# A retention layer and two feed-forward layers on one core: first loads split in two, small tables through ScalarE's queue, decay factors per chunk, eight warm-up matmuls

## The chip, the cores and the metric

The kernel runs on one core of one Trainium2 chip. The metric is the device time of one execution in microseconds (us); of several executions the median is taken. One further execution was recorded by the hardware profiler: its span is the time from its first to its last profiled instruction. The engines are called as in the profile: PE (TensorE matmuls), PEld (its weight loads), DVE (VectorE), ACT (ScalarE), POOL (GpSimd) and SP (SyncE, which here only issues DMA transfers). A q behind a name (SPq, PEq) is the sequencer of that engine, which issues transfers and waits on semaphores.

## The reference, cut to what matters

Inputs are q, k and v of shape (4, 8, 576, 64) and the weights of two feed-forward layers. Everything is float32.

```
scores = (1/8) * q @ k^T                            # per batch and head, 576 x 576
Dmat   = gamma[h] ** (i - j) where i >= j, else 0   # gamma[h] = 1 - 2**(-5-h)
x      = (scores * Dmat) @ v                        # -> 2304 tokens x 512
h      = x @ w_in ;  x = (h * cos(h)) @ w_out       # 512 -> 2048 -> 512
xn     = x / sqrt(mean(x*x) + 1e-6) * rms_g
out    = (silu(xn @ w_gate) * (xn @ w_val)) @ w_out # 512 -> 1536 -> 512
```

## The kernel before

The attention with decay is computed in chunks. Each of the 4 batches of 576 positions has 4 full chunks of 128 positions and a rest of 64, which makes 20 chunks, numbered from 0; chunks 0 to 4 are the first batch. For one chunk the kernel loads four blocks of 128 x 512: `x[:, 0]` is k and `x[:, 1]` is q, both with the head dimension on the partitions, `x[:, 2]` is v and `x[:, 3]` is k again with the tokens on the partitions. In DRAM the four blocks lie side by side in each of the 128 rows, so that one partition's share of a chunk is one piece of 8 KB.

There are three small tables: `gk` (30 KB; decay factors of v in its first part, and in its second, `later`, one factor per head pair and chunk), `mask` (64 KB) and `gq` (256 KB, decay factors of q for the first chunk, which land in `gam0`). The factors of a later chunk c are `gam0` times a scalar from `later`; ScalarE makes them with four multiplications per chunk.

`scores(n)` multiplies v by its factors on POOL (L244), makes the products k q on PE into PSUM tiles `g` (L249), and masks them on DVE into `s` (L252). `values(n)` adds k v of this chunk to the running sum `total` in PSUM (L265), multiplies q by the `state` of the chunks before (L270, from the second chunk on), lets ScalarE copy `total` into `state` (L275), multiplies the masked scores by v (L280), and lets DVE multiply the result by the factors into `xall` (L283). The `g` tiles share three PSUM buffers. `total` of chunk n+1 is accumulated in the bank that the state copy of chunk n reads, so that the first L265 matmul of chunk 1 waits for the state copy of chunk 0.

Ahead of everything stand `WARM` matmuls on a tile of ones (`idle_bank`, L290), whose result nobody reads. The weights of the first feed-forward layer come in blocks of 1 MB (`raw`), and each is converted in several steps by ACT (L132, L141, L159) and DVE (L136, L137, L142, L143, L124). The first of these conversions, and the first products with them (L187 to L189), run between the chunks. That is also where the first layer's activation h cos(h) begins (L414 to L423). From the end of this mixed stage on the kernel is a long row of matmuls for the two feed-forward layers.

Up to the sixteenth step of the first feed-forward layer a scheduler puts the instructions of each engine into an order at build time, out of what it takes to be ready; the order in which the Python code calls the operations is only a priority there. Every engine then executes its own list strictly in that order, and waits on semaphores. Transfers go out in the order of the issuing engine's list, on 8 semaphores in turn: a transfer waits at issue until the one that last used its semaphore has landed. Before the change all transfers are issued by SP.

Of the kernel before, what the change touches and what calls it, by code (L numbers as in the profile page):

```python
# [22 lines left out]
F32 = mybir.dt.float32  # L23
# [3 lines left out]
AF = mybir.ActivationFunctionType  # L27
# [3 lines left out]
P = 128  # L31
# [6 lines left out]
NPAIR = H // 2  # L38
NFULL = S // P
REST = S - NFULL * P  # L40
NCH = NFULL + 1
# [18 lines left out]
NSLOT_B = NW1 - NSLOT_A  # L60
ATT_STEPS = 8
CONV_LEAD = 3
WARM = 10
AHEAD = 4
LAG = 3
LAST_BEGINS = [48, 51, 54, 65, 66, 67]
# [9 lines left out]
def body(ctx: ExitStack, tc, qkv, qkr, vr, w1, w2, rg, gq, gk, mask, out):  # L76
    nc = tc.nc
# [31 lines left out]
    def ps_tile():  # L109
        if "psh" not in late:  # L110
            return psa.tile([P, 512], F32, tag="g", bufs=3, name="g")
        taken[0] += 1
        return hidden_tile() if taken[0] % 2 else acc_tile(KC + taken[0] // 2 % 2)

    mask_sb = const.tile([P, P], F32, name="mask_sb")
# [51 lines left out]
    def temps():  # L167
        return cvp.tile([P, 2, 512], I32, tag="w", name="t")
# [6 lines left out]
    def split_x(t):  # L175
        t0, n = TILES[t]
        for kc in range(KC):
            hi = xsp.tile([P, 512], F32R, tag="xs", name="xhi")
            lo = xsp.tile([P, 512], F32R, tag="xs", name="xlo")
            src = xall[:, kc, t0:t0 + n]  # L180
            nc.scalar.copy(hi[:, :n], src)
            minus(nc.vector, lo[:, :n], hi[:, :n], src)
            xs[t, kc] = (hi, lo)
# [17 lines left out]
    ap1 = att.enter_context(tc.tile_pool(name="ap1", bufs=1, reuse_waits="tile"))  # L201
# [3 lines left out]
    width = lambda c: P if c < NFULL else REST  # L205
    ld, sc, total = {}, {}, {}
    gam0 = ap1.tile([P, NPAIR, P], F32, name="gam0")
    gam = [gam0]
    PRO = NCH
    gk_sb = ap1.tile([P, NCH * (H + NPAIR)], F32, name="gk_sb")  # L210
    vg_sb = gk_sb[:, :NCH * H].rearrange("p (c h) -> p c h", c=NCH)
    later = gk_sb[:, NCH * H:].rearrange("p (c a) -> p c a", c=NCH)
# [6 lines left out]
    def load(n):  # L219

        b, c = chunks[n]
        x = wa.tile([P, 4, DM], F32, tag="w", name="x")
        if n == 0:
            for src, dst in ((qkv[b, c, :, 0], x[:, 0]), (qkv[b, c, :, 1], x[:, 1]), (gk, gk_sb), (mask, mask_sb),
                             (qkv[b, c, :, 2], x[:, 2]), (gq, gam0), (qkv[b, c, :, 3], x[:, 3])):
                nc.sync.dma_start(dst, src)
        elif c < NFULL:
            nc.sync.dma_start(x, qkv[b, c])
        else:
            nc.sync.dma_start(x[:, :2, :NPAIR * REST], qkr[b])  # L230
            nc.sync.dma_start(x[:REST, 2], vr[b])
        blocks = lambda a: a[:, :NPAIR * width(c)].rearrange("p (a i) -> p a i", a=NPAIR)
        ld[n] = blocks(x[:, 0]), blocks(x[:, 1]), x[:, 2], x[:, 3]
        if 0 < n < NCH:
            gam.append(ap1.tile([P, NPAIR, width(c)], F32, name=f"gam{c}"))
            for p in range(NPAIR):
                nc.scalar.activation(gam[c][:, p, :], gam0[:, p, :width(c)], AF.Copy, scale=later[:, c, p:p + 1])

    def scores(n):
        b, c = chunks[n]  # L240
        w = width(c)
        kt, qt, vv, _ = ld[n]
        v3 = vv[:w].rearrange("p (h d) -> p h d", h=H)
        nc.gpsimd.tensor_tensor(v3, v3, vg_sb[:w, c, :].unsqueeze(2).to_broadcast([w, H, D]), op=ALU.mult)  # L244
        ps = [ps_tile().rearrange("p (h i) -> p h i", h=NPAIR) for _ in range(2)]
        for p in range(NPAIR):
            for hh in range(2):
                r = slice(hh * D, (hh + 1) * D)
                nc.tensor.matmul(ps[hh][:w, p, :w], kt[r, p, :], qt[r, p, :], start=True, stop=True)  # L249
        for hh in range(2):  # L250
            s = ap.tile([P, NPAIR, P], F32, tag=f"s{hh}", bufs=2, name=f"s{hh}")
            nc.vector.tensor_tensor(s[:w, :, :w], ps[hh][:w, :, :w],  # L252
                                    mask_sb[:w, :w].unsqueeze(1).to_broadcast([w, NPAIR, w]), op=ALU.mult)
            sc[n, hh] = s

    def values(n):
        b, c = chunks[n]
        w = width(c)
        _, qt, vv, kk = ld.pop(n)
        if c < NFULL:  # L260
            if c == 0:
                total[0] = psa.tile([P, NPAIR, P], F32, tag="st", name="total")
            for p in range(NPAIR):
                cs = slice(p * P, (p + 1) * P)
                nc.tensor.matmul(total[0][:, p, :], kk[:, cs], vv[:, cs], start=c == 0 and p == 0, stop=True,  # L265
                                 skip_group_check=True)
        po = ps_tile().rearrange("p (a i) -> p a i", a=NPAIR)
        if c > 0:
            for p in range(NPAIR):
                nc.tensor.matmul(po[:, p, :w], state[:, p, :], qt[:, p, :], start=p == 0, stop=False,  # L270
                                 skip_group_check=True)
        if c < NFULL:
            for hh in range(2):
                r = slice(hh * D, (hh + 1) * D)
                nc.scalar.copy(state[r, :, r], total[0][r, :, r])  # L275
        for p in range(NPAIR):
            for hh in range(2):
                h = 2 * p + hh
                r = slice(hh * D, (hh + 1) * D)
                nc.tensor.matmul(po[r, p, :w], vv[:w, h * D:(h + 1) * D], sc[n, hh][:w, p, :w],  # L280
                                 start=c == 0 and p == 0, stop=True, skip_group_check=True)
        t0 = b * S + c * P
        nc.vector.tensor_tensor(xall[:, :, t0:t0 + w], po[:, :, :w], gam[c], op=ALU.mult)  # L283
        del sc[n, 0], sc[n, 1]
# [3 lines left out]
    idle_bank = psp.tile([P, 512], F32, tag="acc0", name="idle_bank")  # L288
    for _ in range(WARM):
        nc.tensor.matmul(idle_bank, ones_r, warm, start=True, stop=True)  # L290
    plan = list(PLAN)

    def fetch(until):

        while plan and until not in ld:
            n = plan.pop(0)
            if n < 0:
                blocks1.append(Block(w1[len(blocks1)], wa))
            else:
                load(n)  # L300
# [3 lines left out]
    for n in range(PRO):  # L304
        fetch(n + AHEAD)
        scores(n + 1)
        values(n)
        if n == 3:
            split_x(ORDER_A[0])
            blocks1[0].convert(temps())  # L310
# [316 lines left out]
    for i in range(LAST + LAG):  # L627
# [12 lines left out]
        if i < LAST:  # L640
            t, f = steps[i]
# [278 lines left out]
```

## Time and profile before

| | |
|---|---|
| median of 3 runs | 930.67 us (929.98 to 932.38) |
| the profiled execution, device time | 928.54 us |
| its span | 926.7 us |
| PE busy in the span | 903.1 us (97%) |
| DVE busy | 619.6 us (67%) |
| ACT busy | 462.2 us (50%) |
| moved by the DMA engines | 163.72 MB, mean 177 GB/s |

Busy shares are means over the whole span; the change touches its first microseconds, which have to be read for themselves. The profiled execution's device time is 1.84 us above its span and 2.13 us below the median.

### The profile page before, as it was taken

Reading aid. Unit: us, or ns where it says so; the run is one execution under the profiler, and the core shown is the slowest. Engines: PE = TensorE matmul, PEld = TensorE weight load, DVE = VectorE, ACT = ScalarE, POOL = GpSimd, SP = SyncE. Lnnn points to the kernel's source line nnn. Section 1 sums busy time; section 2 is a strip of 40 time slices with the busy share of each in tenths; the row PEclk is TensorE's granted clock in tenths of the full one; section 3 lists DMA queues with packets and bytes.
Section 4 is the critical chain, followed back from the end, with each engine's and each line's share of the span. In section 5 each row is a group of like instructions: output and inputs, shape, how many; then the busy total and the mean of one; then the engine's idle time right before and its main releaser. Section 6 shows DMA issues by size and latency. Waiting matters only on the chain.

```text
span 926.7 us, 12891 instructions
## 1 busy us (share of the span) xinstructions
PE 903.1 (97%) x4996; PEld 791.0 (85%) x4996; DVE 619.6 (67%) x1022; ACT 462.2 (50%) x816; POOL 26.9 (3%) x27
## 2 busy tenths in 40 slices
PE   7999999999999999999999899999999999999998
PEld 6777788888887888988888799999888999999997
DVE  3999989778888887768657666675456446333332
ACT  4656566576556666367545444444432334322222
POOL 2321100000000000000000000000000000000000
PEclk9999999999999999999999999999999999999999
DMA  8946451035424353202035376676744555755531
GB/s 334 410 186 227 155 224 72 21 117 193 164 98 159 137 159 126 69 1 103 1 148 204 124 297 251 252 268 246 259 176 176 207 209 212 265 206 209 204 132 69
DMA packets 34732, 163.72 MB, mean 177 GB/s; under 512 B 4080, under 2 KB 5232, under 8 KB 23792
## 3 DMA queue, kind: packets, MB, share of 16 engines
q1 hardware_dynamic: 34672, 162.91, 48.0%
q8 instruction: 39, 0.64, 0.3%
q14 instruction: 21, 0.17, 0.1%
HBM read 123.57 MB, written 39.32 MB: 176 GB/s over the span
## 4 chain that ended last, share of the span: by engine, by line
PE 79%; DVE 14%; ACT 4%; issue 2%; DMA 1%; SPq 0%; ACTq 0%; DVEq 0%
PE h L743 27%; PE acc L715 15%; PE acc L187 8%; PE acc L188 8%; PE acc L189 8%; PE h L189 3%; PE h L188 3%; PE h L187 3%; DVE r L421 1%; DVE t L142 1%; DVE t L143 1%; PE g L280 1%; DVE r L415 1%; PE g L249 1%; PE g L270 1%
## 5 line engine op out<-in xcount | busy, mean ns | idle before, releaser
L743 PE MATMUL h<-w 128*128 128x384 f32 x1224 | 230.5, 337 | 6.6 <-ACT s L750 2.6
L743 PEld LDWEIGHTS h<-w 128*128 128x128 f32 x1224 | 214.9, 188 | 15.2 <-ACT s L750 5.3
L715 PE MATMUL acc<-w,shi 128*128 128x512 f32 x432 | 134.3, 392 | 0.0
L187 PE MATMUL acc<-ghi,w 128*128 128x512 f32 (+1 forms) x320 | 117.4, 373 | 2.8 <-ACT xall L614 1.7
L188 PE MATMUL acc<-glo,w 128*128 128x512 f32 (+1 forms) x320 | 117.6, 369 | 0.1
L189 PE MATMUL acc<-ghi,w 128*128 128x512 f32 (+1 forms) x320 | 117.3, 368 | 0.0
L750 ACT COPY s<-h 128x384 f32<-128x384 f32 x108 | 51.9, 480 | 128.1 <-PE h L743 128.0
L715 PEld LDWEIGHTS acc<-w,shi 128*128 128x128 f32 x432 | 80.1, 188 | 13.4
L417 ACT ACTIVATE r<-r,half_pi 128x512 f32<-128x512 f32 (+1 forms) x80 | 54.5, 681 | 65.5 <-DVE r L415 65.2
L763 DVE TENSOR_TENSOR sg<-s,h 128x384 f32<-128x384 f32 x54 | 29.9, 553 | 85.6 <-PE h L743 45.4
L715 PE MATMUL acc<-w,slo 128*128 128x512 f32 x216 | 85.4, 395 | 0.0
L775 ACT CAST shi<-v 128x384 fp32r<-128x384 f32 x72 | 37.0, 514 | 70.3 <-DVE v L771 70.3
L124 DVE TENSOR_TENSOR glo<-r,ghi 128x512 fp32r<-128x512 f32 (+1 forms) x78 | 49.6, 636 | 33.4 <-ACT ghi L423 31.6
L187 PEld LDWEIGHTS acc<-ghi,w 128*128 128x128 f32 x320 | 59.4, 188 | 14.5 <-ACT xall L614 2.8
L423 ACT CAST ghi<-r 128x512 fp32r<-128x512 f32 (+1 forms) x80 | 46.2, 577 | 48.2 <-DVE r L421 46.9
L189 PEld LDWEIGHTS acc<-ghi,w 128*128 128x128 f32 x320 | 60.3, 188 | 10.1
L188 PEld LDWEIGHTS acc<-glo,w 128*128 128x128 f32 x320 | 60.3, 188 | 10.1 <-DVE glo L124 0.3
L124 DVE TENSOR_TENSOR slo<-v,shi 128x384 fp32r<-128x384 f32 x72 | 40.1, 557 | 37.3 <-ACT shi L775 37.3
L770 DVE TENSOR_TENSOR v<-s,h 128x384 f32<-128x384 f32 x54 | 29.8, 552 | 52.0 <-PE h L743 37.9
L743 PE MATMUL h<-b,w 128*128 128x384 f32 x288 | 56.8, 338 | 0.0
L188 PE MATMUL h<-xlo,w 128*128 128x512 f32 (+1 forms) x148 | 54.3, 367 | 0.1
L189 PE MATMUL h<-xhi,w 128*128 128x512 f32 (+1 forms) x148 | 54.2, 366 | 0.0
(105 smaller groups left out, 1518.6 us busy)
## 6 DMA issues: line engine op xcount, KB each, us to landing
w<-s SPq DMA_DIRECT2D x24, 1024.0 KB, 4.8
raw<-w_dram SPq DMA_DIRECT2D x36, 512.0 KB, 4.0
w<-w SPq DMA_DIRECT2D x18, 1024.0 KB, 5.1
w<-s SPq DMA_DIRECT2D x24, 768.0 KB, 6.4
raw<-w_dram SPq DMA_DIRECT2D x16, 1024.0 KB, 7.1
x<-qkv_dram SPq DMA_DIRECT2D x15, 1024.0 KB, 8.1
s<-w SPq DMA_DIRECT2D x12, 1024.0 KB, 4.8
s<-w SPq DMA_DIRECT2D x12, 768.0 KB, 3.6
```

Of the source, the lines that this page charges most:

```text
L124: eng.tensor_tensor(dst, src, hi.bitcast(F32), op=ALU.subtract)
L187: nc.tensor.matmul(dst, a[0], b[0], start=start, stop=False)
L188: nc.tensor.matmul(dst, a[0], b[1], start=False, stop=False)
L189: nc.tensor.matmul(dst, a[1], b[0], start=False, stop=stop)
L417: nc.scalar.activation(r, r, AF.Sin, bias=half_pi, scale=1.0)
L423: nc.scalar.copy(hi, r)
L715: nc.tensor.matmul(acc, (hi, hi, lo)[k][:, c], w[:, u, (0, 1, 0)[k], :], start=start and u == 0 and k == 0, stop=stop and u == 1 and k == 2)
L743: nc.tensor.matmul(bank, a[:, wp], xp[:, c], start=start and kc == 0 and n == 0, stop=kc == 1 and n == 2, skip_group_check=True)
L750: nc.scalar.copy(t, alpha)
L763: nc.vector.tensor_tensor(t, s, bank, op=ALU.add)
L770: nc.vector.tensor_tensor(t, s, bank, op=ALU.add)
L775: nc.scalar.copy(hi, t)
```

## The change

The first chunk's four blocks come in two transfers of two blocks each, in place of four; the second chunk's come in two in place of one. The three tables are issued by ScalarE (`nc.scalar`) in place of SP. The four multiplications that make a chunk's decay factors are called when the previous chunk has been computed, in a function of their own, and no longer at the load. `WARM` is 8 in place of 10.

```diff
-WARM = 10
+WARM = 8
...
         if n == 0:
-            for src, dst in ((qkv[b, c, :, 0], x[:, 0]), (qkv[b, c, :, 1], x[:, 1]), (gk, gk_sb), (mask, mask_sb),
-                             (qkv[b, c, :, 2], x[:, 2]), (gq, gam0), (qkv[b, c, :, 3], x[:, 3])):
-                nc.sync.dma_start(dst, src)
+            for eng, src, dst in ((nc.sync, qkv[b, c, :, :2], x[:, :2]), (nc.scalar, gk, gk_sb),
+                                  (nc.scalar, mask, mask_sb), (nc.sync, qkv[b, c, :, 2:], x[:, 2:]),
+                                  (nc.scalar, gq, gam0)):
+                eng.dma_start(dst, src)
+        elif n == 1:
+            nc.sync.dma_start(x[:, :2], qkv[b, c, :, :2])
+            nc.sync.dma_start(x[:, 2:], qkv[b, c, :, 2:])
         elif c < NFULL:
             nc.sync.dma_start(x, qkv[b, c])
...
-        if 0 < n < NCH:
-            gam.append(ap1.tile([P, NPAIR, width(c)], F32, name=f"gam{c}"))
-            for p in range(NPAIR):
-                nc.scalar.activation(gam[c][:, p, :], gam0[:, p, :width(c)], AF.Copy, scale=later[:, c, p:p + 1])
+
+    def decay(c):
+
+        gam.append(ap1.tile([P, NPAIR, width(c)], F32, name=f"gam{c}"))
+        for p in range(NPAIR):
+            nc.scalar.activation(gam[c][:, p, :], gam0[:, p, :width(c)], AF.Copy, scale=later[:, c, p:p + 1])
...
         fetch(n + AHEAD)
         scores(n + 1)
         values(n)
+        if n + 1 < NCH:
+            decay(n + 1)
```

The scheduler puts the following rows at the start of ScalarE's list; before the change first (`gam` are the decay factors, `gam_91` the loaded table, `raw` and `t` belong to the first weight block):

```order
L237 ACT_TABLE_LOAD
L237 ACTIVATE gam_121<-gam_91,gk_sb 128x128 x4
L237 ACTIVATE gam_143<-gam_91,gk_sb 128x128 x4
L237 ACTIVATE gam_150<-gam_91,gk_sb 128x128 x4
L237 ACTIVATE gam_160<-gam_91,gk_sb 128x64 x4
L275 COPY state<-total 64x4x64 x4
L132 ACTIVATE t<-raw 128x1024
```

After the change ScalarE's list begins as follows (its line 243 is line 237 of before, and 281 is 275):

```order
L227 DMA gk_sb<-gk_dram 128x60
L227 DMA mask_sb<-mask_dram 128x128
L227 DMA gam_91<-gq_dram 128x512
L243 ACT_TABLE_LOAD
L243 ACTIVATE gam_174<-gam_91,gk_sb 128x128 x4
L243 ACTIVATE gam_216<-gam_91,gk_sb 128x128 x4
L243 ACTIVATE gam_260<-gam_91,gk_sb 128x128 x4
L243 ACTIVATE gam_302<-gam_91,gk_sb 128x64 x4
L281 COPY state<-total 64x4x64 x4
L132 ACTIVATE t<-raw 128x1024
```

Three transfers now stand ahead; the sixteen multiplications stand together as before, ahead of the first state copy, although they are called chunk by chunk.

PE's list begins so before the change (L249 are the scores, L265 the sum k v, L280 the masked scores times v):

```order
L290 MATMUL idle_bank<-warm,ones_r 128x512 x10
L249 MATMUL g<-x 128x128 x8
L265 MATMUL total<-x 128x128 x4
L249 MATMUL g<-x 128x128 x8
L280 MATMUL g<-s_137,x 64x128
...
L265 MATMUL total<-x 128x128 x2
L249 MATMUL g<-x 128x128 x8
L265 MATMUL total<-x 128x128 x2
L270 MATMUL g<-x,state 128x128 x4
```

And so after it (255 is 249, 271 is 265, 276 is 270, 286 is 280):

```order
L296 MATMUL idle_bank<-warm,ones_r 128x512 x8
L255 MATMUL g<-x 128x128 x16
L271 MATMUL total<-x 128x128 x4
L286 MATMUL g<-s_129,x 64x128
...
L271 MATMUL total<-x 128x128 x4
L255 MATMUL g<-x 128x128 x8
L276 MATMUL g<-x,state 128x128 x4
```

The scores of chunk 1 moved ahead of the sum of chunk 0, and the sum of chunk 1 is no longer split around the scores of chunk 2.

In DVE's list the rows of the first weight block and of chunks 2 to 5 stand so before the change:

```order
L252 TENSOR_TENSOR s_251<-g,mask_sb 128x512
L136 TENSOR_SCALAR t<-t 128x1024
L137 TENSOR_SCALAR t<-t 128x1024
L142 SCALAR_TENSOR_TENSOR t<-raw,t 128x1024
L283 TENSOR_TENSOR xall<-g,gam_143 128x4x128
L252 TENSOR_TENSOR s_286<-g,mask_sb 64x4x64
L252 TENSOR_TENSOR s_288<-g,mask_sb 64x4x64
L143 ISA t<-raw,t 128x2048
L283 TENSOR_TENSOR xall<-g,gam_150 128x4x128
```

And so after it (258 is 252, 289 is 283):

```order
L258 TENSOR_TENSOR s_238<-g,mask_sb 128x512
L136 TENSOR_SCALAR t<-t 128x1024
L137 TENSOR_SCALAR t<-t 128x1024
L289 TENSOR_TENSOR xall<-g,gam_216 128x4x128
L258 TENSOR_TENSOR s_278<-g,mask_sb 64x4x64
L258 TENSOR_TENSOR s_280<-g,mask_sb 64x4x64
L142 SCALAR_TENSOR_TENSOR t<-raw,t 128x1024
L143 ISA t<-raw,t 128x2048
L289 TENSOR_TENSOR xall<-g,gam_260 128x4x128
```

One step of the weight conversion moved behind three steps of the attention. Differences of this kind, a conversion step or a few matmuls that stand some places earlier or later, go on through the first quarter of DVE's list, the first fifth of ACT's and the first sixth of PE's; behind that the lists are the same.

## Rows read from the trace of the kernel before

**Rows 1.** The page: the span, and busy time of each engine.

```profile
span 926.7 us, 12891 instructions
PE 903.1 (97%) x4996; PEld 791.0 (85%) x4996; DVE 619.6 (67%) x1022; ACT 462.2 (50%) x816; POOL 26.9 (3%) x27
```

**Rows 2.** Windows: length, busy time (instructions) by engine, granted clock, DMA share, GB/s.

```profile
10.00:15.00 5.00, 2.59 (x36) 2.10 (x35) 1.89 (x3) 4.58 (x17) 2.08 (x2) 1.00 1.01 428
15.00:20.00 5.00, 5.00 (x64) 4.45 (x63) 1.98 (x3) 1.57 (x3) 1.04 (x1) 1.00 1.05 377
20.00:25.00 5.00, 4.92 (x61) 4.27 (x57) 4.72 (x7) 2.10 (x4) 2.62 (x2) 1.00 0.99 413
...
30.00:60.00 30.00, 27.37 (x212) 22.45 (x213) 29.36 (x37) 18.22 (x26) 7.19 (x6) 0.94 0.83 328
...
130.00:160.00 30.00, 30.00 (x136) 24.79 (x133) 29.64 (x39) 21.84 (x28) 0.00 (x0) 1.00 0.40 158
```

**Rows 3.** The chain that ended last, two pieces: start, length, what.

```profile
3.07 4.95 DMA gam<-gq_dram
...
14.75 0.68 PE total L265 x4
```

**Rows 4.** The timeline of the first 23 us: start, length, instruction [idle before <- releaser].

```profile
0.74 0.87 SPq L226 DMA_DIRECT2D x<-qkv_dram  x2
...
2.10 4.59 PE L290 MATMUL idle_bank<-warm,ones_r 128*128 128x512 f32 x10 [2.10 <-DVE warm L287]
...
3.07 0.43 SPq L226 DMA_DIRECT2D gam<-gq_dram  x1
...
4.02 1.54 SPq L228 DMA_DIRECT2D x<-qkv_dram  x3
...
6.62 1.16 PE L249 MATMUL g<-x 64*128 64x128 f32 x16
7.44 1.04 POOL L244 TENSOR_TENSOR x<-x,gk_sb 128x512 f32<-128x512 f32 x1 [6.51 <-DMA x<-qkv_dram]
...
8.10 1.28 ACT L237 ACT_TABLE_LOAD   x1 [8.10 <-DMA gam<-gq_dram]
...
9.03 1.13 PE L265 MATMUL total<-x 128*128 128x128 f32 x8 [1.25 <-DMA x<-qkv_dram]
9.39 4.57 ACT L237 ACTIVATE gam<-gam,gk_sb 128x128 f32<-128x128 f32 x16
...
11.48 1.16 PE L249 MATMUL g<-x 64*128 64x128 f32 x16 [1.32 <-DMA x<-qkv_dram]
...
12.57 1.09 PE L280 MATMUL g<-s,x 128*64 128x128 f32 x16
...
14.75 0.68 PE L265 MATMUL total<-x 128*128 128x128 f32 x4 [1.09 <-ACT state L275]
...
19.16 1.15 ACT L132 ACTIVATE t<-raw 128x1024 f32<-128x1024 f32 x1 [0.25 <-DMA raw<-w_dram]
...
22.25 0.76 ACT L275 COPY state<-total 64x256 f32<-64x256 f32 x2 [0.88 <-PE g L270]
```

**Rows 5.** DMA issues in short windows: size, us from issue to landing.

```profile
x<-qkv_dram SPq DMA_DIRECT2D x1, 256.0 KB, 3.0
...
gam<-gq_dram SPq DMA_DIRECT2D x1, 256.0 KB, 5.0
...
x<-qkv_dram SPq DMA_DIRECT2D x1, 1024.0 KB, 7.4
...
raw<-w_dram SPq DMA_DIRECT2D x1, 1024.0 KB, 13.5
```

**Rows 6.** Windows of 1 us in the first load phase (columns as in Rows 2).

```profile
2.00:3.00 1.00, 0.90 (x2) 0.83 (x3) 0.00 (x0) 0.00 (x0) 0.00 (x0) 1.00 0.75 260
...
5.00:6.00 1.00, 1.00 (x3) 0.79 (x3) 0.00 (x0) 0.00 (x0) 0.00 (x0) 1.00 0.87 203
```

**Rows 7.** One window with a lower granted clock (columns as in Rows 2).

```profile
33.90:37.30 3.40, 3.40 (x9) 2.63 (x9) 3.33 (x6) 0.17 (x1) 1.05 (x1) 0.51 1.03 411
```

## The prediction

> **What bounds the kernel now.** I read the page first. PE is busy for 903.1 of 926.7 us [rows 1], so all that any change can take out of this kernel, short of taking work from PE, is the 23.6 us in which PE has nothing to do. The question is how much of that lies where the change is made. The windows tell it. From 15 to 20 us PE is busy for the whole 5.00 us, and from 130 to 160 us for all of 30.00; in between DVE is the one that is full, with 29.36 of 30 us from 30 to 60 us [rows 2]. Before 15 us it is otherwise: from 10 to 15 us PE works for 2.59 us and DVE for 1.89, while ACT works for 4.58 [rows 2]. So the start is a stage of its own, and ends when PE becomes full at about 14.75 us.
>
> The chain of waits says what sets that moment. It goes from the issue of the table `gq` at 3.07 us, by its transfer of 4.95 us, through ACT to the matmul L265 that starts chunk 1's sum at 14.75 us [rows 3]. The timeline has the pieces: the table has landed at about 8.05 us, ACT loads its function table (8.10, 1.28 us), makes all sixteen products for the decay factors (9.39, 4.57 us), and only then, in the order of its list, copies the state, which the L265 row at 14.75 us names as its releaser [rows 4]. From landing to L265 that is 14.75 - 8.05 = 6.70 us. Everything else that chunk 1 needs stands ready: its scores ended at 12.64 us and L280 of chunk 0 at 13.66 [rows 4].
>
> From there each chunk hands on to the next, and nothing is tied to the clock on the wall but what the transfers bring. So if L265 of chunk 1 starts earlier by some amount, PE's full stretch starts earlier by that amount, DVE's full stretch behind it too, and so the end, as long as data and order allow. That is the sum that I make: the shift of this one moment.
>
> **The change part by part.**
>
> The tables through ScalarE. SP issues seven transfers of 0.42 to 0.44 us each for chunk 0 and the tables, and `gq` is the sixth, at 3.07 us [rows 4]. Now it is third in ACT's own list. If ACT starts at the same 0.74 us and needs the same time for an issue, `gq` goes out at 0.74 + 2 x 0.43 = 1.6 us. How long it then takes, no row shows, since ACT issues no transfer before. From below: the first `x` transfer has the same 256 KB and finds the engines empty, 3.0 us [rows 5], which gives 4.6 us. From above: `gq`'s own 5.0 us with five transfers ahead [rows 5], which gives 6.6. It will share the engines with 512 KB of chunk 0 ahead of it and 512 KB beside it, so neither row is clearly nearer, and I take the middle, 5.6 us. L265 then starts at 5.6 + 6.70 = 12.3 us in place of 14.75: a gain of 2.45 us, with 3.45 and 1.45 as its ends.
>
> Against the tables' new queue stands a rule of the Trainium skill, in the page "DMA: Bandwidth & Descriptors", section "Issuing engines are not separate DMA queues": transfers started by different engines run on the same 16 DMA engines and mix there, and a second issuing engine saves only the time of issue. By that rule the gain is at its lower end, 3.07 - 1.6 = 1.45 us, since only the issue moves.
>
> The decay factors per chunk. By the code ACT would make four products, copy the state, and go on. By the order it does not: all sixteen stand ahead of the first copy as before. This edit costs and gives nothing. Had it worked, twelve products (3.4 us of the 4.57) would have left the path, and PE's own work would have set the time.
>
> The loads in two transfers. x of chunk 0 goes out in two issues in place of four, and with the tables gone SP has issued chunk 0 and the whole of chunk 1 by 0.74 + 4 x 0.43 = 2.5 us; before, chunk 1 was issued at 4.02 us and landed 7.4 us later, at 11.4 [rows 4, 5]. In the first load phase, with rows of 2 KB and smaller, the engines moved 260 and 203 GB/s [rows 6], some 230; with rows of 8 KB they moved 428 [rows 2]. Rows of 4 KB do not occur before, so I take these as bounds. The first half of chunk 1 is ready when 1.57 MB of x and at most 0.36 MB of tables have moved from about 1.75 us on, the second half with 0.52 MB more: with some 0.5 us until the landing is seen, 6.8 to 10.6 us and 8.0 to 12.9 us. That this is early enough decides whether the 2.45 us stand. PE, in the new order, does the scores of chunk 0, the scores of chunk 1, the sum of chunk 0 and L280 of chunk 0, of 1.16, 1.16, 1.13 and 1.09 us [rows 4]: with the first half landed at 6.8 us it is done at 10.2, at 10.6 us at 14.0. POOL needs 1.04 us [rows 4] behind the second half, 9.0 to 13.9. In the middle of the ranges PE is done at 12.1 and POOL at 11.5, and ACT, at 12.3, is last, if by little. So the loads earn nothing by themselves, but cover the tables; at the slow end L265 would start at 14.0 us and the gain would shrink to 0.7 us.
>
> The first weight block sits behind the loads. It lands at 5.6 + 13.5 = 19.1 us, and ACT takes it up at 19.16 [rows 4, 5]; behind it on ACT stands the state copy of chunk 2, which today has 0.88 us of idle time before it [rows 4]. With 5.6 MB moved, of which 2.1 MB at 330 GB/s (the middle), 0.36 MB at 230 and 3.1 MB at 428, it now lands at about 17.4 us, 1.7 us earlier. With the 0.88 us this allows a shift of up to 2.6. The 2.45 just fit.
>
> Eight warm-up matmuls. Ten take 4.59 us [rows 4], so two are worth 0.9 us of PE time before the scores of chunk 0, which can begin at about 5.8 us. PE's path has 12.3 - 10.2 = 2.1 us of slack if chunk 1 is early, and waits for its transfer if it is late. Nothing comes of this edit either way, but for the clock, below.
>
> The new order behind 15 us. Some conversion steps and matmuls change places in a stretch in which PE and DVE are both close to full: from 30 to 60 us PE has 2.6 us free and DVE 0.6 [rows 2]. DVE's work is the same, so a gain is bounded by about that 0.6 us and what PE loses to a slow clock there; a loss is not bounded by a row. I put it at 0, and allow 1.5 us on either side, about half of PE's free time there.
>
> Sum: -2.45 us. The profiled execution would go from 928.54 to 926.1 us; set against the median, which is 2.13 us above that execution, 930.67 becomes **928.2 us**.
>
> **The rivals.** What a measurement of this kernel can tell from no change is about 0.3%, 2.8 us.
>
> First, small gain. The tables gain only their earlier issue, or chunk 1 comes late, or the new order gives a microsecond back. For it speaks that the engines are already 75 to 87% busy in the first load phase [rows 6], so that `gq` has to share with x wherever it is issued. The gain is 0.7 to 1.45 us, in the middle 1.1: 929.6 us.
>
> Second, larger gain. `gq` meets the lower end (3.45 us earlier), and the new order closes some of the 2.6 us of PE's holes from 30 to 60 us, among them the stretch from 33.9 to 37.3 us at a granted clock of 0.51, in which nine matmuls ran where the row from 130 to 160 us has 136 in 30 us, or 15 in 3.4 [rows 2, 7]: 926.3 us. Against it: the conversion of the first weight block allows about 2.6.
>
> Third, slower, by the clock. The granted clock fell to the lower level, 1.2 GHz, at 33.9 us, after a stretch in which PE had waited for ACT and DVE [rows 7]; and the ten warm-up matmuls went at 0.46 us each [rows 4] against 0.22 later [rows 2], so they ran at the lower level too, though the clock column has 1.00 there. With two fewer of them, and with chunk 1's scores now ahead of chunk 0's sum, PE may stand idle from about 7 us until the first half of chunk 1 lands. If the clock then stays at 1.2 GHz, the 9.3 us of matmuls from the scores of chunk 0 to L280 of chunk 1, which ended at 19.1 us, run at half pace until it rises at a time T, and end at 12.2 + T/2. Even with before is T = 13.8 us; 2.8 us slower, T = 19.4. At that point the time would be 933.5 us. Against it: before, PE idled for 1.09 to 1.32 us three times by 14.75 us [rows 4] and the clock held at 1.00 [rows 2]. The page "TensorE: Matmul & The Clock Gate" of the Trainium skill says, in its part 1, that the low clock is the idle state and that matmul activity lifts it; the trace agrees with the 0.46 and 0.22 us above.
>
> That the change does not do what it says holds for the decay factors, as said; it is in the sum.
>
> **How the numbers follow.** The forecast, a gain of 1.7 to 3.3 us, gets 0.42, the larger gain 0.24, the small one 0.22, slower or no gain by clock or order 0.12. The forecast's own range is 927.4 to 929.0 us; the part of it beyond 2.8 us is the smaller one, so 0.16 of the 0.42 counts as faster. Faster by over 0.3%: 0.16 + 0.24 = 0.40. Slower by over 0.3%: 0.08 of the 0.12. Within: 0.52. The range leaves out the far ends of the larger gain and most of slower: 925.0 to 931.4 us.
>
> **What would show it.** Right: in the changed trace `gq` lands near 5.6 us, the first state copy ends near 12.2 and names the last decay product ahead of it, L265 of chunk 1 starts near 12.3, and PE and DVE do at 27 us what they did at 30. The table load waits for `gq` alone. The two transfers of chunk 1 land by about 8.7 and 10.4 us. Wrong: L265 waits for POOL or a transfer; ACT stands before the weight block with the state copy behind it; a granted clock of 0.5 in the first 20 us; or PE's idle time from 20 to 130 us differs by more than 1.5 us, which would say that the order and not the start decided.

## The result, and the profile after

The changed kernel is slower: 937.97 us median of 6 runs (935.78 to 938.81) against 930.62 us (927.10 to 932.38), a ratio of 1.0076 [1.0059, 1.0094]. The forecast was 928.2 us (925.0 to 931.4). The profiled execution took 938.81 us, and its page begins so:

```profile
span 937.0 us, 12888 instructions
...
PE 907.4 (97%) x4994; PEld 794.7 (85%) x4994; DVE 621.5 (66%) x1022; ACT 462.0 (49%) x816; POOL 27.7 (3%) x27
```

The span is 10.3 us longer than in [rows 1], and PE is busy for only 4.3 us more. The rest is idle time of PE, so something waits. Some 3 us of the 10.3 belong to the two executions that were profiled: the one of before took 2.1 us less than its median, this one 0.8 us more than its own. The first place to look is where the change was made. The timeline of the changed kernel, its first 20 us (start, length, what, and in brackets the idle time before and what ended it):

```profile
1.62 0.45 ACTq L227 DMA_DIRECT2D gam<-gq_dram  x1
...
5.78 1.87 PE L255 MATMUL g<-x 64*128 64x128 f32 x16
...
8.57 1.28 ACT L243 ACT_TABLE_LOAD   x1 [8.57 <-DMA gam<-gq_dram]
9.02 1.16 PE L255 MATMUL g<-x 64*128 64x128 f32 x16 [1.37 <-DMA x<-qkv_dram]
...
9.87 4.57 ACT L243 ACTIVATE gam<-gam,gk_sb 128x128 f32<-128x128 f32 x16
...
14.34 0.74 ACT L281 COPY state<-total 64x256 f32<-64x256 f32 x2
15.18 1.13 PE L271 MATMUL total<-x 128*128 128x128 f32 x8 [2.89 <-issue]
...
19.36 1.15 ACT L132 ACTIVATE t<-raw 128x1024 f32<-128x1024 f32 x1
```

The table `gq` is issued at 1.62 us, as forecast, but ACT gets it only at about 8.5 us, where before it had it at 8.05 [rows 4]. From there the start runs as the prediction said, with all sixteen products in one row ahead of the state copy, and L271 of chunk 1 (L265 before) starts at 15.18 us in place of 14.75. The transfers of the first 25 us say why (KB each, median us from issue to landing):

```profile
gam<-gq_dram ACTq DMA_DIRECT2D x1, 256.0 KB, 6.9
...
mask_sb<-mask_dram ACTq DMA_DIRECT2D x1, 64.0 KB, 4.9
```

The table took 6.9 us from ScalarE's queue, where it took 5.0 from SP's [rows 5]. Its issue 1.45 us earlier is more than given back. Still, 0.4 us at the start is not 10. The windows (length, busy time and instructions of PE, PEld, DVE, ACT, POOL, granted clock, DMA share, GB/s) tell where the rest is:

```profile
10.00:15.00 5.00, 2.29 (x28) 1.82 (x24) 1.98 (x3) 4.97 (x18) 2.08 (x2) 1.00 1.01 426
15.00:20.00 5.00, 4.82 (x58) 4.32 (x59) 1.66 (x3) 1.45 (x4) 1.38 (x2) 1.00 1.04 364
20.00:25.00 5.00, 5.00 (x67) 4.52 (x64) 4.25 (x9) 2.29 (x4) 1.74 (x2) 1.00 1.00 418
...
30.00:60.00 30.00, 23.24 (x158) 18.36 (x160) 29.15 (x34) 16.95 (x23) 7.77 (x6) 0.92 0.73 281
60.00:90.00 30.00, 28.68 (x236) 23.68 (x235) 23.21 (x32) 15.73 (x24) 2.33 (x2) 0.85 0.50 176
```

Up to 25 us the rows look like those of before [rows 2]. From 30 to 60 us PE is busy for 23.24 us against 27.37, while DVE is full in both; from 60 to 90 us the clock is 0.85, where the same window of before has 29.96 us of PE at 1.00:

```profile
60.00:90.00 30.00, 29.96 (x267) 24.69 (x263) 28.82 (x39) 20.77 (x28) 4.61 (x4) 1.00 0.53 181
```

Over both windows PE is idle for 8.1 us against 2.7, which is 5.4 more, and the clock takes 0.08 x 30 + 0.15 x 30 = 6.9 us against 1.8, which is 5.1 more. Together 10.5 us: by this reckoning as much as the whole difference of the two spans lies between 30 and 90 us, where the prediction had put 0. The view of the waits names what PE waits for from 20 to 130 us (total, times, longest):

```profile
PE g L276 <- DVE s L258: 6.0, 3, 3.6
PE g L286 <- DVE s L258: 1.9, 1, 1.9
```

L258 is the masking of the scores on DVE (L252 before). The same view of before has these two kinds (L280 and L270 there) at 1.2 and 0.4 us:

```profile
PE g L280 <- DVE s L252: 1.2, 1, 1.2
...
PE g L270 <- DVE s L252: 0.4, 1, 0.4
```

The longest of them in the timeline, DVE and PE rows:

```profile
50.32 1.54 DVE L136 TENSOR_SCALAR t<-t 128x1024 f32<-128x1024 f32 x1
51.78 1.22 DVE L124 TENSOR_TENSOR w<-t,w 128x1024 fp32r<-128x1024 f32 x1
...
52.91 1.53 DVE L137 TENSOR_SCALAR t<-t 128x1024 int32<-128x1024 int32 x1
...
54.48 1.22 DVE L142 SCALAR_TENSOR_TENSOR t<-raw,t 128x1024 int32<-128x1024 int32 x1
55.62 0.68 DVE L423 SCALAR_TENSOR_TENSOR r<-r,g 128x512 f32<-128x512 int32 x1
56.22 1.22 DVE L143 CUSTOM_DVE_ANT_0 t<-raw,t 128x2048 uint16<-128x2048 uint16 x1
...
57.36 1.28 DVE L258 TENSOR_TENSOR s<-g,mask_sb 128x512 f32<-128x512 f32 x2
...
58.09 1.74 PE L276 MATMUL g<-x,state 128*128 128x128 f32 x8 [3.65 <-DVE s L258]
```

DVE is hardly idle here; it converts the fourth weight block, and the two masks, the 17th and 18th of its list, stand behind that. PE stands for 3.65 us, until the first of the two is done at about 58.0 us. Its next product by its own list, L276, multiplies q by the state and reads no masked scores. By the program what it lacks is one of the three `g` buffers to write into, and a mask that has read its scores sets one free; the view names only the mask as the releaser. So the 6.0 us of L276 are waits for a buffer, and the 1.9 us of L286, which multiplies the masked scores by v, are a wait for the masked scores themselves. Right behind the 3.65 us, a window of the changed kernel from 58.0 to 61.4 us shows the granted clock at 0.57, so PE was for most of it at the lower of its two levels, 1.2 GHz:

```profile
58.00:61.40 3.40, 3.31 (x24) 3.02 (x24) 2.38 (x4) 1.94 (x5) 0.00 (x0) 0.57 0.76 282
```

### The profile page after: what moved, and what is told of

Its sections match the earlier page's. It is cut to its first block, busy times and chain, and to the rows that moved or that the text cites. A ratio compares the mean times of both kernels' runs of the same rounds, so it can differ in the third digit from the quotient of the medians.

```text
span 937.0 us, 12888 instructions
## 1 busy us (share of the span) xinstructions
PE 907.4 (97%) x4994; PEld 794.7 (85%) x4994; DVE 621.5 (66%) x1022; ACT 462.0 (49%) x816; POOL 27.7 (3%) x27
## 4 chain that ended last, share of the span: by engine, by line
PE 71%; DVE 19%; ACT 5%; issue 3%; DMA 1%; SPq 0%; POOL 0%; ACTq 0%; DVEq 0%
PE h L751 26%; PE acc L723 15%; PE acc L187 6%; PE acc L189 6%; PE acc L188 6%; DVE t L142 2%; DVE r L429 2%; PE h L187 2%; PE h L188 2%; PE h L189 2%; DVE r L423 2%; DVE t L143 2%; DVE glo L124 2%; ACT ghi L431 2%; PE g L286 1%
## 5 line engine op out<-in xcount | busy, mean ns | idle before, releaser
L189 PEld LDWEIGHTS acc<-ghi,w 128*128 128x128 f32 x320 | 60.3, 188 | 10.2
```

The costliest lines, as they stand in the source:

```text
L189: nc.tensor.matmul(dst, a[1], b[0], start=False, stop=stop)
```

## The experiments

Four theories had to be told apart. **Order**: the engines' lists behind the start, which the scheduler made anew, put DVE's conversion steps ahead of masks that PE waits for. **Queue**: the tables on ScalarE's queue land late. **Transfers**: the loads in halves disturb what comes behind. **Warm-up**: with two warm-up matmuls fewer PE gets the full clock late. In several of the experiments the scheduler changed its lists again; what they became is in the table. "Changed" lists are those of the changed kernel, "old" ones those of before. Every kernel has the reference's whole work in it.

The two last columns are means over all timed executions of a kernel. Each is recorded with its span and its mean granted clock; clock loss is span x (1 - clock), and the rest, span x clock, is an estimate of what the execution would have taken at the full clock throughout. The clock is recorded to 0.001, which is 0.9 us of one span. The kernel before has 3.8 to 4.2 us and 924.9 to 925.3 us in the three sets of executions that were timed beside the experiments (26 to 31 each), and medians of 930.79, 930.95 and 931.63 us.

| kernel | lists | `gq` issued by, landed | median us | ratio to before [95%] | clock loss | rest |
|---|---|---|---|---|---|---|
| changed | changed | ScalarE, 8.5 us | 937.97 | 1.0076 [1.0059, 1.0094] | 8.1 | 927.5 |
| e1_warm10 | changed | ScalarE, 9.0 | 937.68 | 1.0076 [1.0046, 1.0107] | 8.2 | 927.9 |
| e2_warm14 | old | ScalarE, 8.9 | 929.90 | 0.9993 [0.9977, 1.0008] | 3.1 | 925.1 |
| e3_halves | old | SP, 8.7 | 930.81 | 1.0001 [0.9985, 1.0016] | 3.1 | 925.7 |
| e4_halves_decay | changed | SP, 7.9 | 934.83 | 1.0041 [1.0022, 1.0060] | 4.5 | 928.1 |
| e5_sp_tables | old | SP, 6.0 | 929.85 | 0.9991 [0.9978, 1.0003] | 3.8 | 924.5 |
| e6_sp_tables_decay | old | SP, 5.9 | 930.78 | 1.0006 [0.9996, 1.0016] | 4.7 | 924.2 |
| e7_changed_sp | changed | SP, 6.0 | 935.68 | 1.0044 [1.0027, 1.0061] | 6.8 | 925.9 |
| e8_masks_first | third | ScalarE, 8.8 | 933.86 | 1.0035 [1.0021, 1.0049] | 3.6 | 927.8 |
| e9_chunk0_alone | fourth | ScalarE, 10.0 | 934.16 | 1.0038 [1.0024, 1.0052] | 5.1 | 927.3 |
| e10_attention_first | fifth | SP, 7.3 | 931.10 | 0.9996 [0.9983, 1.0009] | 3.0 | 926.0 |
| e11_changed_att | sixth | ScalarE, 9.1 | 935.34 | 1.0048 [1.0030, 1.0066] | 4.8 | 928.6 |
| e12_sp_att | sixth | SP, 5.8 | 931.09 | 0.9999 [0.9985, 1.0012] | 3.0 | 926.0 |

"Old" and "changed" mean that DVE's list is that one; in e2, e3 and e6 a handful of PE's or ACT's rows stand otherwise, e12's lists differ from e11's by as few, and e4's ACT list has the state copy ahead of the last five products.

**e1_warm10, e2_warm14: the warm-up, and the order by chance.**

```diff
-WARM = 8
+WARM = 10
```

This is e1; e2 has 14 there.

> The changed kernel with ten warm-up matmuls again in place of eight; every engine's list is otherwise row for row that of the changed kernel. Theory of the lists (the seven microseconds come from the order that the scheduler now gives DVE and PE between 30 and 90 us, in which PE waits for masked scores): 938 us, 0.7 to 0.9% over the kernel before, PE waiting 1.9, 3.6 and about 1.3 us for masked scores as in the changed kernel. Theory of the warm-up (two matmuls fewer leave PE's clock to fall): back to within 0.3% of 930.6 us, one stretch at the lower clock as before. Theory of the transfers (tables and halves of chunks land at a worse time): 938 us.

> The changed kernel with fourteen warm-up matmuls. All transfers are issued as in the changed kernel, but the scheduler then gives DVE exactly the list of the kernel before, and PE and ACT that list but for a handful of rows. Theory of the lists: within 0.3% of the kernel before, 929 to 932 us, although the large table still lands near 8.5 us. Theory of the transfers: 938 us as the changed kernel. Theory of the warm-up: also back to before, so that it is told from the lists by the run with ten.

With ten warm-ups, as before the change, the changed kernel is as slow as with eight. With fourteen the scheduler returns to before's list on DVE, with all of the changed transfers in place, and the time is before's. From e1 to e2 that is 7.8 us. The table lands at 8.9 us in e2, and chunk 1's sum starts later than in the changed kernel, at 15.57 us:

```profile
15.57 0.68 PE L271 MATMUL total<-x 128*128 128x128 f32 x4 [2.69 <-issue]
```

So with the old lists neither the late table nor the transfers cost anything that shows. The DVE rows of e2 at the same place of the list, again the fourth weight block and the 17th and 18th mask, which now stand between the conversion steps:

```profile
51.08 1.53 DVE L136 TENSOR_SCALAR t<-t 128x1024 f32<-128x1024 f32 x1
52.54 0.68 DVE L258 TENSOR_TENSOR s<-g,mask_sb 128x512 f32<-128x512 f32 x1
53.14 1.21 DVE L124 TENSOR_TENSOR w<-t,w 128x1024 fp32r<-128x1024 f32 x1
54.27 1.53 DVE L137 TENSOR_SCALAR t<-t 128x1024 int32<-128x1024 int32 x1
55.72 0.68 DVE L258 TENSOR_TENSOR s<-g,mask_sb 128x512 f32<-128x512 f32 x1
56.32 1.21 DVE L142 SCALAR_TENSOR_TENSOR t<-raw,t 128x1024 int32<-128x1024 int32 x1
57.45 0.67 DVE L423 SCALAR_TENSOR_TENSOR r<-r,g 128x512 f32<-128x512 int32 x1
58.05 1.21 DVE L143 CUSTOM_DVE_ANT_0 t<-raw,t 128x2048 uint16<-128x2048 uint16 x1
```

The steps are the same and nearly as long; the two masks come 4.8 and about 2.2 us earlier. And the windows of e2:

```profile
30.00:60.00 30.00, 26.14 (x221) 21.60 (x218) 29.14 (x37) 19.09 (x26) 7.47 (x6) 1.00 0.80 299
60.00:90.00 30.00, 29.93 (x254) 24.99 (x255) 27.22 (x38) 19.22 (x27) 4.37 (x4) 0.94 0.53 189
```

e2 has four warm-ups more as well, but they are no shield for the clock: from 15 to 20 us it is 0.71 in its profile, and the time is before's all the same. A low clock in the first 20 us does not decide: it is also 0.69, 0.66 and 0.51 from 10 to 15 us in the profiles of e3, e6 and e10, whose times are before's, and 1.00 in the changed kernel's. No run has fourteen warm-ups with the changed lists, so it takes the next pair, with ten in both, to part the order from the matmuls that brought it.

**e3_halves, e4_halves_decay: order against transfers, from before's side.** Both start from the kernel before; e4 has e3's transfers and the decay factors per chunk.

```diff
+        elif n == 1:
+            nc.sync.dma_start(x[:, :2], qkv[b, c, :, :2])
+            nc.sync.dma_start(x[:, 2:], qkv[b, c, :, 2:])
```

This is e3; e4 has it too, and calls the function `decay` of the change where the change calls it:

```diff
+        if n + 1 < NCH:
+            decay(n + 1)
```

> The kernel before with one edit: the second chunk is loaded in two transfers. The lists are those of before but for a few PE rows at the start. Theory of the lists: within 0.3% of 930.6 us. Theory of the transfers: some of the seven microseconds appear, 2 us or more over before.

> The run with the second chunk in two transfers, and one edit more: the decay factors are called chunk by chunk. Same transfers on the same queue, ten warm-up matmuls; but the scheduler now gives DVE the list of the changed kernel, row for row. Theory of the lists: 937 to 939 us, as the changed kernel, 7 us over its twin with one edit. Theories of the warm-up and of the transfers: no different from its twin, 930 to 931 us.

e3 costs nothing. e4, with the same transfers, tables on SP and ten warm-ups, gets the changed kernel's list on DVE, and is 4.0 us slower than e3, although its start is better: the state copy stands behind eleven products in place of sixteen, and chunk 1's sum starts at 13.31 us. The 4.0 us are less than the 7 that the theory of the order had put there, and more than the nothing of the others. The waits of e4:

```profile
PE g L275 <- DVE s L257: 3.8, 1, 3.8
...
PE g L285 <- DVE s L257: 2.2, 2, 1.9
```

The masks (L257 here) come late again. The theory of the order holds on two pairs, and the one of the transfers falls.

**e5_sp_tables, e6_sp_tables_decay, e7_changed_sp: the queue.** The tables stay on SP's queue, with `gq` third, right behind `gk`. e5 is before's kernel with this alone; e6 adds the decay factors per chunk and eight warm-ups; e7 is the changed kernel with it.

```diff
+            for src, dst in ((qkv[b, c, :, :2], x[:, :2]), (gk, gk_sb), (gq, gam0), (mask, mask_sb), (qkv[b, c, :, 2:], x[:, 2:])):
+                nc.sync.dma_start(dst, src)
```

> The kernel before with one edit: the first chunk in two transfers, and the tables still on SyncE's queue but the large one third, ahead of the mask and of the first chunk's second half. Every engine's compute list is row for row that of before. Theory that ScalarE's queue was what held the large table back: it now lands near 6 us in place of 8.5 in the changed kernel, and chunk 1's sum starts near 13.2 us, when PE's own path to it is done. If an earlier start is passed on to the end, as the prediction had it, the time falls by about 1.4 us, to 929.3; rival: the gain is taken up by DVE's full stretch and nothing is measured. In both cases within 0.3% of before; the profile tells by when PE and DVE do the same row at 30 and at 130 us.

> The run before this one with two edits more: decay factors chunk by chunk, and eight warm-up matmuls. Here the scheduler lets the first state copy follow five products and not sixteen; DVE's and PE's lists stay those of before but for the warm-ups. Expected: first state copy by 10.5 us, chunk 1's sum at about 13.0 us, bound by PE and chunk 1's transfer. Theory of the lists: no loss, 928.5 to 930 us. Theory of the warm-up: eight matmuls cost, 933 us or more.

> The changed kernel with the tables back on SyncE's queue, the large one third. DVE's list is row for row that of the changed kernel. Theory of the lists: still 935 to 938 us, although the table lands near 6 us and the first state copy is done by 11 us, so that chunk 1's sum starts 1.5 to 3 us earlier than in the changed kernel. Theory of the transfers and of ScalarE's queue: back to 930 us or below.

On SP's queue, third, `gq` lands at 6.0 us in e5, 4.3 us after its issue, so what the change set out to gain is there. e5 has before's lists exactly. Its chunk 1 starts 1.1 us earlier than before's. That is a test of the prediction's main step, that an earlier start is passed on to the end. The timeline of e5 shows what became of it:

```profile
13.63 0.71 PE L264 MATMUL total<-x 128*128 128x128 f32 x4
...
20.27 1.16 ACT L132 ACTIVATE t<-raw 128x1024 f32<-128x1024 f32 x1 [2.45 <-DMA raw<-w_dram]
...
22.51 0.76 ACT L274 COPY state<-total 64x256 f32<-64x256 f32 x2
23.41 1.13 PE L264 MATMUL total<-x 128*128 128x128 f32 x8 [0.71 <-ACT state L274]
...
26.38 2.08 PE L269 MATMUL g<-x,state 128*128 128x128 f32 x8 [1.84 <-DVE xall L282]
```

ACT comes to the first weight block early, waits 2.45 us for its transfer, and the next state copy stands behind that in its list; PE then waits for the copy and for `xall`, 2.55 us in all. The 1.1 us are gone by 27 us. The time is 0.9991 [0.9978, 1.0003], no gain that can be told from none. e6 has 1.0006 with before's list on DVE: there the decay factors per chunk and the eight warm-ups cost nothing that shows, so that e4's loss is not the decay edit's own.

e7 has the changed kernel's list on DVE, the table at 6.0 us, and is still 1.0044. Its windows:

```profile
30.00:60.00 30.00, 22.34 (x162) 17.51 (x162) 29.37 (x34) 17.00 (x23) 7.29 (x6) 0.94 0.75 297
60.00:90.00 30.00, 30.00 (x245) 25.21 (x242) 22.48 (x33) 17.14 (x25) 2.88 (x3) 0.84 0.49 174
```

So the bad order costs with an early table too. An early start it had not, in its profile: chunk 1's sum starts at 15.21 us there and not the 1.5 to 3 us earlier that were expected, with the clock at 0.50 from 10 to 15 us. Between the changed kernel and e7 lie some 0.3%; that the queue has a part in the loss with these lists is likely, but the two were not timed side by side.

**e8_masks_first, e10_attention_first, e11_changed_att, e12_sp_att: mending the order.** The scheduler is told to prefer the masks (e8, on the changed kernel), or the masks, the state copies and the products into `xall` (e10 on before, e11 on the changed kernel, e12 on e7).

```diff
+            with tc.high_priority():
                 nc.vector.tensor_tensor(s[:w, :, :w], ps[hh][:w, :, :w],
                                         mask_sb[:w, :w].unsqueeze(1).to_broadcast([w, NPAIR, w]), op=ALU.mult)
...
+                with tc.high_priority():
                     nc.scalar.copy(state[r, :, r], total[0][r, :, r])
...
+        with tc.high_priority():
             nc.vector.tensor_tensor(xall[:, :, t0:t0 + w], po[:, :, :w], gam[c], op=ALU.mult)
```

> The changed kernel with the masking of the scores at the highest priority in the scheduler; transfers and warm-ups as in the changed kernel. The lists are new ones: the masks stand some rows earlier among the weight conversions between 30 and 90 us. If it is the masks behind conversion steps that cost, PE's waits for masked scores from 20 to 130 us fall from 7.9 to under 4 us, and the time from 938 to 930 to 934 us. If it is only that lists differ at all from the old ones, 936 us or more.

> The kernel before, transfers and warm-ups unchanged, with the masking, the state copies and the products into the layer's input at the highest priority in the scheduler. If it were a rule that attention steps belong ahead of the weight conversions, this is no slower than before and faster by up to 2 us, 928 to 931. If the old lists were merely a lucky set, 932 us or more.

> The changed kernel with the same three kinds of attention steps at the highest priority; its transfers and eight warm-ups unchanged. By the theory that conversion steps ahead of attention steps cost the seven microseconds, 930 to 933 us, PE's waits for DVE from 20 to 130 us under 4 us and at most two stretches at the lower clock. If masks and their priority are not the point, 935 us or more.

> The run of the changed kernel with its tables on SyncE (large one third), with the same attention steps at the highest priority. The table lands near 6 us. If an earlier start is passed on at all once the lists do no harm, this is 1 to 2 us faster than its twin with the tables on ScalarE's queue, and the best candidate to beat before: 928 to 931 us. If it is taken back at the first weight block, no faster than its twin.

The first of the three edits is e8's, all three are in the others. e8 takes back about half: PE's waits for masks at the products with the state come to 2.8 us in place of 6.0, and the clock loss falls from 8.1 to 3.6 us, no more than before's, while the rest stays at 927.8 us. e10, the attention steps first in the kernel before, gains nothing that shows. e11 came out against its theory: PE's waits for masks are down to 2.1 us in its profile, as they are to 2.0 in e12's, and the time is still 935.34 us, where 930 to 933 were expected. So late masks do not explain e11. e11 and e12 have the same lists but for a few rows and differ in the tables' queue: 1.0048 and 0.9999, timed side by side, 4.3 us apart. In e11 the table load waits until 9.13 us, in e12 until 5.83 us; chunk 1's sum starts at 15.74 and 13.72 us. The timeline of e11, and then of e12:

```profile
9.13 1.28 ACT L243 ACT_TABLE_LOAD   x1 [9.13 <-DMA gam<-gq_dram]
...
15.74 2.04 PE L272 MATMUL total<-x 128*128 128x128 f32 x8 [3.83 <-issue]
...
22.64 1.15 ACT L132 ACTIVATE t<-raw 128x1024 f32<-128x1024 f32 x1
```

```profile
5.83 1.28 ACT L241 ACT_TABLE_LOAD   x1 [5.83 <-DMA gam<-gq_dram]
...
13.72 1.16 PE L270 MATMUL total<-x 128*128 128x128 f32 x8
...
18.48 1.14 ACT L132 ACTIVATE t<-raw 128x1024 f32<-128x1024 f32 x1 [0.57 <-DMA raw<-w_dram]
```

Here the queue costs, more than the 2.0 us by which the start moves: with the rest, 2.6 us, goes 1.8 us of clock. In e11's profile PE is idle for the 3.83 us up to 15.74 us, and the clock is at the lower level until after 20 us:

```profile
15.00:20.00 5.00, 4.26 (x25) 3.84 (x26) 0.17 (x1) 0.62 (x2) 1.42 (x2) 0.50 1.04 365
```

The same window of e12 has 5.00 us of PE at 1.00, and so ACT takes up the first weight block at 22.64 us in e11, 4.2 us behind e12. These are single executions, and e1, with the changed lists, looks like e11 there (0.50, and 22.43 us). With the old lists the queue costs nothing (e2 beside e5, 0.9993 and 0.9991). That an early start is worth something only where the order lets it through is the reading of both, not a test; no run put the early table, the early weight blocks and the old lists together, since with chunk 1 split and `gq` third on SP's queue (e7) the scheduler gave the changed list.

**e9_chunk0_alone: the edit of chunk 0 by itself on before**, two transfers for its x, the tables through ScalarE, ten warm-ups and the decay factors as before.

> The kernel before with the first chunk's part of the change alone: two transfers, and the tables through ScalarE. Ten warm-up matmuls, second chunk in one transfer, decay factors at the load. The scheduler then gives a third set of lists, unlike those of before and of the changed kernel. The large table is again expected near 8.5 us. Theory of the lists: the time is that of this third set, and is told by PE's waits for DVE behind 30 us: with under 4 us of them 930 to 932, with 8 us 937. Theory of ScalarE's queue: slower than before by the 0.4 to 0.8 us that the table lands later, 931 us.

It gives yet another set of lists and 1.0038, with the largest single wait for masks of all profiles, 5.3 us, of 6.1 us in all from 20 to 130 us. The table took 8.4 us after issue. Time and waits both lie between what its expectation had put for good and for bad lists, and order and queue are not parted in this run.

No version beats before by more than its interval; e5 comes nearest.

## Why the prediction was wrong

**The step that failed** is "The new order behind 15 us": "I put it at 0, and allow 1.5 us on either side". The forecast is 9.8 us too low: 2.45 us of gain did not come, which is the table's part, below, and 7.35 us of loss came, and this step had them at 0. The pairs with the same transfers and other lists say 7.8 us (e1 and e2) and 4.0 us (e4 and e3), and every kernel with the changed list on DVE is slower than before by more than its interval, while none of the four with the old list is. How much of the 7.35 us needs the late table as well stays open: with an early one e7 lost 4.7. The prediction saw that a loss "is not bounded by a row" and then bounded it, by half of PE's free time, which is a bound on a gain. It had in its hand that DVE was full from 30 to 60 us [rows 2]: on a full engine every step that moves ahead of a mask delays it by its whole length, 0.7 to 1.5 us for one conversion step, and PE behind the mask, for the masked scores or for the `g` buffer. The rows of DVE's list that stand ahead of the prediction are those at the first weight block, where masks had moved ahead; the block that cost most is the fourth, at 50 to 58 us.

How the loss splits into waits and clock was read, not tested. Over all executions the changed kernel has 4.1 us more of clock loss than before (8.1 against 3.8 to 4.2) and 2.4 us more of the rest. The three low stretches from 30 to 90 us (0.50 from 42 to 44 us, 0.57 from 58.0 to 61.4, 0.50 from 76 to 82) come behind PE's three longest waits for masks, of 1.93, 3.65 and 1.32 us, ended at 40.08, 58.09 and 73.43 us; but a wait of 1.34 us before 57.86 us in the kernel before was not followed by one. e8 lost the clock's part with the shorter waits. No run held PE's waits and changed the clock. The split is not the same everywhere: against the kernel before timed beside it, e4 has 0.7 us more of clock loss and 3.2 us more of the rest, e7 has 2.6 and 1.0. And the waits cost without the clock too: the six of e4's ten executions at 0.995 or 0.996 average 934.88 us, where the eleven of before at the same clock average 930.86 us. The prediction's slower rival was right in that the clock would fall, and wrong in its place: it looked at the first 20 us, which are at 1.00 in the changed kernel's profile. The page "TensorE: Matmul & The Clock Gate" of the Trainium skill, part 1, which it named there, has the low clock as the idle state; the 3.65 us of idle PE before 58.09 and the 0.57 behind agree with it.

**The table.** "I take the middle, 5.6 us" for the landing was mis-sized: 8.5 us in the changed kernel, outside of both ends, 4.6 and 6.6. From ScalarE's queue it took 6.9 to 8.4 us in six profiles. The upper end was taken from a transfer on the one busy queue and did not bound one on a second queue. So L265's start at 12.3 us was 15.18 us. The Trainium skill's rule in "DMA: Bandwidth & Descriptors", section "Issuing engines are not separate DMA queues", that only the time of issue is saved, was nearer than the forecast; the runs show less than it grants, since the 1.45 us of issue were saved and 0.5 us of landing were lost.

**Passing the start on.** "if L265 of chunk 1 starts earlier by some amount, PE's full stretch starts earlier by that amount [...] and so the end, as long as data and order allow": in e5 data and order did not. There 1.1 us of earlier start ended at ACT's wait for the first weight block, the very place for which the prediction had named a cover of 0.88 us; in e5 the block lands at about 20.2 us, later than the 19.1 of before. In the changed kernel it was taken up at 19.36 us without a wait, so there the cover held, but no earlier start used it. What an early start is worth behind an early block and in before's order stays open.

**Right** were: the decay edit leaves the sixteen products in one row and gives nothing at the start (that it costs nothing holds with the old lists, e6; in e4 it is what brings the new ones); the warm-ups are worth nothing (e1, e6); from the table's landing to chunk 1's sum it takes 6.6 us (6.70 forecast); the first weight block, issued at 4.92 us, landed 12.9 us later, at 17.8 us (17.4); chunk 0's scores begin at 5.78 us (5.8 forecast); chunk 1's halves, issued at 1.66 and 2.14 us, landed at about 9.0 and 10.2 us (8.7 and 10.4). The test that it set itself at its end, PE's idle time from 20 to 130 us, is the one that told: 110.00 - 100.78 = 9.2 us in the changed kernel, 4.7 before. The windows, changed first:

```profile
20.00:130.00 110.00, 100.78 (x869) 83.10 (x866) 100.97 (x128) 60.11 (x84) 19.82 (x16) 0.94 0.57 215
```

```profile
20.00:130.00 110.00, 105.30 (x936) 87.36 (x932) 103.65 (x133) 64.80 (x92) 19.33 (x16) 0.98 0.62 237
```

## What to carry to other kernels

Where a scheduler makes the lists, an edit of a load is two changes, the transfer and a new order on every engine, and they have to be priced apart: here the first was worth nothing that shows with the old lists, the second 4.0 and 7.8 us of 930 in the two pairs, and six more matmuls on a tile of ones gave the old order back. The two need not add up: with a third order (e11, e12) the table's queue was worth 4.3 us. Compare the whole list of the fullest engine before and after, and for each instruction that someone waits for, for its result or for the buffer that it sets free, count the time of what now stands ahead of it. To test such a change, look for a second edit that restores the old order with the new transfers in place; the pair gives the price of each.

## What was not expected of the hardware

The 256 KB of `gq` took 6.9 to 8.4 us from issue to landing through ScalarE's queue beside SP's x transfers, and 4.1 to 4.4 us as the third transfer on SP's own queue (e5, e6, e7, e12). The `mask` of 64 KB, on ScalarE's queue ahead of it, took 4.9 to 5.6 us, as against 3.9 to 4.1 on SP's behind it, so it is not this one transfer alone that was late. By 8.5 us of the changed kernel the transfers of SP's queue had moved 1.80 MB and those of ScalarE's 0.36 MB. Only 1.05 MB of x, chunk 0's, were issued ahead of `gq`, so some 0.7 MB issued after it on the other queue passed before it had landed. Its place differs too: third on SP's queue it has 0.55 MB ahead of it. How much of the difference is the queue and how much the place was not parted, since no run has the same place on both.

Within one kernel the executions differ by their clock: in e4 the two of ten with a mean granted clock of 0.998 took 930.80 and 930.90 us, and the six at 0.990 to 0.995 took 934.39 to 937.15 us. A part of the scatter that one sees between runs of a kernel like this one is PE's clock.
